# Sliding-window attention and RWKV channel mix on one core: batch 3 joins the batches that are transposed by the DMA crossbar, with a new instruction order

## The chip, the core and the metric

The kernel runs on one core of a Trainium2 chip. The metric is the device time of one execution in microseconds (us), and of several executions their median. One further execution was recorded by the hardware profiler; it has a time of its own and a span, which is the part of it between the first and the last recorded instruction. The engines are named as the profile names them: PE (matrix multiply, with PEld for its weight loads), DVE (vector), ACT (scalar and activation), POOL (GpSimd, here mostly an issuer of software DMAs) and SP (sync, an issuer of hardware DMAs).

## The reference

The input is q, k and v of 8 batches, 8 heads, 576 positions and 64 channels, in float32. The output has the shape (8, 576, 512).

```python
scores = q @ k.T / 8                     # per batch and head, 576 x 576
rel    = i - j
scores = where(0 <= rel < 128, scores - slope[h] * abs(rel), -1e9)
attn   = softmax(scores)
x      = (attn @ v).transpose(0, 2, 1, 3).reshape(8, 576, 512)

x_prev = x shifted by one position (zero at the start of a batch)
xk = mu_k * x + (1 - mu_k) * x_prev
xr = mu_r * x + (1 - mu_r) * x_prev
k  = relu(xk @ w_k) ** 2                 # w_k: 512 x 1024
v  = k @ w_v                             # w_v: 1024 x 512
r  = sigmoid(xr @ w_r)                   # w_r: 512 x 512
out = r * v
```

## The kernel before

**Attention.** A batch is worked on in two halves `c` of four heads, and each half in two groups, so that a batch has four groups `g` of two heads. Matrix operands are bf16. POOL loads q and k with software DMAs as they lie into one of two `raw` buffers (L561, four loads a batch: q and k of each half), and v into one of two `vs` buffers (L540, L545). DVE turns `raw` into `qt` with 32x32 block transposes (L1150, four a batch from batch 1 on). PE makes the scores in 32-row tiles (L1173, function `scores4`), ACT takes the exponential (L1190), DVE multiplies by the mask, which holds window and ALiBi factors (L1200). PE multiplies with v (L796, function `attend`), DVE takes the reciprocal of the sums (L802) and writes the scaled result of a group, positions on the partitions, to one of four `xu` buffers (L807).

**From positions to channels.** The channel mix needs x with its channels on the partitions, in one of two `xt` buffers (one for even batches, one for odd). There are two ways from `xu` to `xt`, and the set `XO` picks the batches of the second. In the first, `out_t`, PE transposes the five 128x128 blocks of a group against an identity matrix into PSUM (L834), and ACT copies the result to `xt` (L710). In the second, `out_flip`, SP issues one DMA that passes through the transposing crossbar, from `xu` to `xt` for all five blocks (L882); the text calls it a flip. In both cases DVE makes the difference of neighbours `dl` (L860) and from it `xk` and `xr` (L867, function `shift`).

**Channel mix.** It works on pairs of batches (0 and 1, 2 and 3, ...), 1152 positions in chunks: 512 when the even batch is there, 384 and 256 when the odd one is; the first pair's 512 are done as 256 and 256. PE multiplies xk by w_k (L949), ACT takes the relu (L956), the square is made on ACT (L920) or DVE (L922), PE multiplies xr by w_r (L967), ACT takes a tanh (L974), from which the sigmoid follows, PE multiplies by w_v (L983), DVE makes the product `ot` (L988), and SP stores rows of 128 positions (L1013); the last 128 columns are stored by ACT (L1007). The number of hardware DMAs, `n_hw`, is rounded up to a multiple of 8 by storing the last rows in two halves each (`n_split` of them).

**The gate.** Ahead of batch b's raw loads, if batch b-2 is in `XO`, POOL copies one element of each group of batch b-2's `xt` to a scratch tile `gap` (L653, function `gate_load`). POOL works in order, so these loads and everything behind them on POOL are held until the flips of batch b-2 have landed.

```python
if GATED and what == "a" and b - 2 in XO:
    gate_load(b)
```

**The order.** All steps are nodes of a list scheduler (class `Plan`) that runs ahead of the launch, in Python. It takes for each engine, whenever that is free by modelled costs, the ready node with the lowest priority value for which buffers are free. Where a node may go to ACT or DVE (the squares, some copies), it goes to the one that the scheduler finds free first. The priority of a node comes from `rank`: its place in the program, moved by tables for each engine (`LEAD` by batch, `SHIFT` by kind of step) and by `NUDGE`, which holds a number for each of some thousand nodes by its running number. `WAIT` puts certain 64-row transposes of PE back, `COST` scales modelled DMA costs, and `FX` is an extra latency that the scheduler adds to the flips of each batch. The engines then carry out exactly the order that the scheduler found, each waiting on semaphores where an operand or a buffer is not there yet. A wrong modelled cost thus shows on the chip as a wait at a fixed place in the order.

Of the kernel before, what the change touches and what calls it, by code (L numbers as in the profile page):

```python
# [182 lines left out]
def kernel(  # L183
# [14 lines left out]
    B, H, S, D = q.shape  # L198
# [16 lines left out]
    XO = range(4,B)  # L215
# [15 lines left out]
    FX = (0, 4, 4, 4, 4, 4, 0, 0)  # L231
# [3 lines left out]
    WAIT = 5.15  # L235
# [90 lines left out]
    def dve_t(n, fast=1):  # L326
# [4 lines left out]
        PE: (379.11, 948.28, 321.48, 777.92, 344.48, 715.92, 627.75, 578.6, 241.8, 354.15),  # L331
        ACT: (700.83, 2.12, 322.35, 108.16, 185.72, -3.46, 340.58, 397.46, 747.05, 580.68),
        DVE: (282.18, -111.4, 162.81, 61.6, 37.49, 18.01, -37.8, -38.84, 70.95, -86.71),
# [3 lines left out]
        PE: {(0, 0): -1189.02, (3, 0): 492.42, (2, 0): 367.63, (1, 0): 298.05, (1, 1): -728.2, (1, 2): 117.95, ('p1', 'fxk'): -1.92, ('rl', 'fp1'): -1166.05, ('frl',): 219.95, ('rs', 'fp1'): 514.38, ('p1', 'fkk'): 4.9, ('fkk',): 426.5, ('ot', 'fp1', 'frs'): 532.6, ('fp1', 'frs'): -626.2},  # L337
        ACT: {(0, 0): -688.81, (3, 0): -610.15, (2, 0): -722.11, (1, 0): 289.16, (1, 1): -432.67, (1, 2): 1038.71, ('p1', 'fxk'): 478.01, ('rl', 'fp1'): 76.23, ('frl',): 491.94, ('rs', 'fp1'): -82.07, ('p1', 'fkk'): -497.1, ('fkk',): 342.85, ('ot', 'fp1', 'frs'): -48.3, ('fp1', 'frs'): 278.04},
        DVE: {(0, 0): -195.31, (3, 0): 34.28, (2, 0): 73.75, (1, 0): 36.73, (1, 1): -73.62, (1, 2): 45.06, ('p1', 'fxk'): 69.74, ('rl', 'fp1'): 265.96, ('frl',): 137.45, ('rs', 'fp1'): -180.96, ('p1', 'fkk'): -389.9, ('fkk',): 250.87, ('ot', 'fp1', 'frs'): -277.33, ('fp1', 'frs'): 509.68},
    }  # L340
    NUDGE = {
# [930 lines left out]
```

## Time and profile before

| | us |
|---|---|
| median of 3 runs | 228.47 |
| lowest, highest | 228.15, 228.95 |
| profiled execution, its time | 227.53 |
| profiled execution, its span | 225.8 |
| PE busy | 217.1 (96%) |
| DVE busy | 196.3 (87%) |
| ACT busy | 166.6 (74%) |
| POOL busy | 59.7 (26%) |

The granted clock of PE was 0.997 of full speed. Busy times of PE count overlapping matmuls up to their modelled ends, so that a stretch in which PE is busy throughout may still have room in it; what an instruction costs PE in a row of others is read from the starts of neighbours in the timeline. In a row of the groups, the columns are the line, engine, operation, operands and count, then the busy time in us and the mean of one in ns, then the idle time ahead of it and what ended that.

### The profile page before, as it was taken

Reading aid. Unit: us, or ns where it says so; the run is one execution under the profiler, and the core shown is the slowest. Engines: PE = TensorE matmul, PEld = TensorE weight load, DVE = VectorE, ACT = ScalarE, POOL = GpSimd, SP = SyncE. Lnnn points to the kernel's source line nnn. Section 1 sums busy time; section 2 is a strip of 40 time slices with the busy share of each in tenths; the row PEclk is TensorE's granted clock in tenths of the full one; section 3 lists DMA queues with packets and bytes.
Section 4 is the critical chain, followed back from the end, with each engine's and each line's share of the span. In section 5 each row is a group of like instructions: output and inputs, shape, how many; then the busy total and the mean of one; then the engine's idle time right before and its main releaser. Section 6 shows DMA issues by size and latency. Waiting matters only on the chain.

```text
span 225.8 us, 5825 instructions
## 1 busy us (share of the span) xinstructions
PE 217.1 (96%) x2339; PEld 128.5 (57%) x2339; DVE 196.3 (87%) x386; ACT 166.6 (74%) x311; POOL 59.7 (26%) x88
## 2 busy tenths in 40 slices
PE   8999978999999999999999999999999999999993
PEld 8576636755756555554774546445674455456542
DVE  7388999999999999999999999999989966983332
ACT  3669999766999789978996796677996684427511
POOL 8776525465100910160007500091000000000000
PEclk9999999999999999999999999999999999999998
DMA  6999999999971997095434995489991315140023
GB/s 157 182 165 195 202 153 207 192 175 233 208 162 49 83 197 179 3 130 88 151 77 58 219 190 108 106 130 188 165 112 29 144 46 121 39 154 37 3 93 139
DMA packets 66298, 29.74 MB, mean 132 GB/s; under 512 B 53976, under 2 KB 58336, under 8 KB 66272
## 3 DMA queue, kind: packets, MB, share of 16 engines
q0 software_dynamic: 46832, 16.26, 66.9%
q1 hardware_dynamic: 17696, 12.53, 20.5%
q10 hardware_dynamic: 1744, 0.59, 1.0%
q8 instruction: 18, 0.29, 0.5%
q14 instruction: 8, 0.07, 0.1%
HBM read 33.56 MB, written 9.44 MB: 190 GB/s over the span
## 4 chain that ended last, share of the span: by engine, by line
PE 80%; DVE 8%; ACT 6%; DMA 3%; issue 1%; SPq 1%; DVEq 0%; ACTq 0%
PE uno L949 25%; PE uno L983 25%; PE uno L967 12%; PE duo L796 7%; PE duo L1173 6%; DMA qx<-in_q_dram 3%; DVE xu L807 2%; DVE qt L1150 2%; ACT at L1190 2%; PE uno L834 2%; PE uno L701 1%; DVE xk L867 1%; ACT mask L1130 1%; ACT at L754 1%; DVE xr L867 1%
## 5 line engine op out<-in xcount | busy, mean ns | idle before, releaser
L949 PE MATMUL uno<-xk,wk_sb 128*128 128x256 bf16 (+2 forms) x416 | 71.3, 314 | 1.7 <-DVE xk L867 1.3
L983 PE MATMUL uno<-wv_sb,kk 128*128 128x512 bf16 (+2 forms) x296 | 68.4, 374 | 0.0
L1190 ACT ACTIVATE at<-duo 128x1024 bf16<-128x1024 f32 x56 | 55.3, 1038 | 12.5 <-PE duo L1173 12.3
L956 ACT ACTIVATE rl<-uno 128x256 bf16<-128x256 f32 (+2 forms) x104 | 47.7, 483 | 14.1 <-PE uno L949 12.8
L949 PEld LDWEIGHTS <-wk_sb 128*128 128x128 bf16 x416 | 38.6, 98 | 24.1 <-issue 3.0
L983 PEld LDWEIGHTS <-kk 128*128 128x128 bf16 x296 | 27.2, 98 | 30.1 <-issue 1.9
L540 POOL DMA_DIRECT2D vs<-in_v_dram x32 | 28.5, 903 | 38.9 <-PE duo L796 29.9
L1200 DVE TENSOR_TENSOR at<-at,mask 128x1024 bf16<-128x1024 bf16 x56 | 37.1, 679 | 1.0 <-ACT at L1190 1.0
L967 PE MATMUL uno<-wr_sb,xr 128*128 128x512 bf16 x144 | 35.9, 379 | 0.0
L974 ACT ACTIVATE rs<-uno 128x512 bf16<-128x512 f32 x36 | 22.0, 618 | 18.5 <-PE uno L967 17.5
L920 ACT ACTIVATE kk<-rl 128x256 bf16<-128x256 bf16 (+2 forms) x67 | 33.7, 530 | 0.8
L1150 DVE STREAM_TRANSPOSE qt<-raw 128x576 f32<-128x576 f32 x28 | 33.7, 1233 | 0.0
L988 DVE SCALAR_TENSOR_TENSOR ot<-rs,uno 128x512 f32<-128x512 bf16 (+2 forms) x37 | 24.0, 663 | 6.7 <-ACT rs L974 4.6
L867 DVE SCALAR_TENSOR_TENSOR xr<-dl,mu_sb,xt 128x576 bf16<-128x576 bf16 (+1 forms) x32 | 24.6, 774 | 0.1
L867 DVE SCALAR_TENSOR_TENSOR xk<-dl,mu_sb,xt 128x576 bf16<-128x576 bf16 (+1 forms) x32 | 24.5, 774 | 0.0
L807 DVE TENSOR_TENSOR xu<-duo,rc 128x640 bf16<-128x640 f32 x28 | 22.8, 818 | 1.5 <-PE uno L834 0.8
L796 PEld LDWEIGHTS <-at 128*128 128x128 bf16 x576 | 21.6, 98 | 4.4 <-issue 0.3
L967 PEld LDWEIGHTS <-xr 128*128 128x128 bf16 x144 | 13.4, 98 | 13.6 <-issue 0.2
L922 DVE TENSOR_TENSOR kk<-rl 128x256 bf16<-128x256 bf16 (+2 forms) x37 | 12.2, 334 | 8.7 <-ACT rl L956 8.0
L796 PE MATMUL duo<-vs,at 128*128 128x65 bf16 x448 | 18.9, 193 | 0.0
L1173 PE MATMUL duo<-qt 32*128 32x256 bf16 (+2 forms) x560 | 18.0, 250 | 0.7 <-ACT at L1190 0.4
L1173 PEld LDWEIGHTS <-qt 32*128 32x128 bf16 x560 | 11.9, 92 | 11.5 <-issue 9.7
(73 smaller groups left out, 160.4 us busy)
## 6 DMA issues: line engine op xcount, KB each, us to landing
out_dram<-ot SPq DMA_DIRECT2D x34, 256.0 KB, 2.8
vs<-in_v_dram POOLq DMA_DIRECT2D x32, 128.0 KB, 10.0
raw<-in_q_dram POOLq DMA_DIRECT2D x14, 288.0 KB, 8.2
raw<-in_k_dram POOLq DMA_DIRECT2D x14, 288.0 KB, 9.3
wk_sb<-in_moe_w_k_dram POOLq DMA_DIRECT2D x2, 512.0 KB, 7.5
wv_sb<-in_moe_w_v_dram POOLq DMA_DIRECT2D x2, 512.0 KB, 11.5
qx<-in_k_dram ACTq DMA_DIRECT2D x4, 128.0 KB, 5.1
qx<-in_q_dram SPq DMA_DIRECT2D x4, 128.0 KB, 4.8
```

The lines of the kernel that those rows point to most:

```text
L540: return dma(POOL, 256, issue_t(1024), lambda e: nc.gpsimd.dma_start(out=vs_buf[h.idx][:, j, :, 0:D], in_=v[b, :, 128 * j:128 * j + 128].r ...
L796: nc.tensor.matmul(a[:, hl, t - t0], lhsT=at[:, lo:lo + 128], rhs=vs[:, u, 2 * g + hl, :] if u < NF else tvb[:, 2 * g + hl], start=(u == u ...
L867: lambda e: nc.vector.scalar_tensor_tensor(out=buf[hk.idx][:, g, e0 + c0:e0 + c1], in0=dls(), scalar=mu[:, g:g + 1], in1=xc(1), op0=ALU.mu ...
L920: nc.scalar.activation(out=out, in_=in_, func=AF.Square)
L949: nc.tensor.matmul(one(hp)[:, 0:n], lhsT=wk_sb[:, po, 128 * fo:128 * fo + 128], rhs=xk_buf[hx.idx][:, po, c0:c1], start=(po == 0), stop=(p ...
L956: a = op(ACT, act_t(n), [s], pr, lambda e, hp=hp, hr=hr: nc.scalar.activation(out=rl_buf[hr.idx][:, 0:n], in_=one(hp)[:, 0:n], func=AF.Rel ...
L967: nc.tensor.matmul(one(hp), lhsT=xr_buf[hx.idx][:, po, 128 * c:128 * c + 128], rhs=wr_sb[:, po], start=(po == 0), stop=(po == NPO - 1))
L983: nc.tensor.matmul(one(hv)[:, a:b], lhsT=kk_buf[hk.idx][:, fo, o:o + 128], rhs=wv_sb[:, fo, a:b], start=(fo == 0), stop=(fo == NFO - 1))
L1150: nc.vector.transpose(out=qt_buf[hq.idx][:, S * i:S * i + S].rearrange("p s t -> p (s t)").bitcast(FP32) .rearrange("p (q t) -> p t q", t=TB),
L1173: nc.tensor.matmul(two(hps[j // 2])[:, j % 2, c0:c0 + n], lhsT=qt[r:r + 32, S + 128 * u:S + 128 * u + 128, t], rhs=qt[r:r + 32, q0:q0 + n, t],
L1190: lambda e, ah=ah, j=j: nc.scalar.activation(out=ah(), in_=two(hps[j]), func=AF.Exp, scale=float(scale)), (), [hps[j]])
L1200: nc.vector.tensor_tensor(out=a, in0=a, in1=m, op=ALU.mult)
```

## The change

Batch 3 joins `XO`: its four groups are transposed by four flips instead of 20 transposes on PE and four copies on ACT. From the rule of the gate it follows that POOL now holds the raw loads of batch 5 until the flips of batch 3 have landed. The scheduler's extra latency `FX` for the flips of batches 1 to 5 becomes 1 us instead of 4, `WAIT` becomes 18.69, and `LEAD`, `SHIFT` and `NUDGE` are replaced as a whole.

```diff
-    XO = range(4,B)
+    XO = range(3,B)
...
-    FX = (0, 4, 4, 4, 4, 4, 0, 0)
+    FX = (0, 1, 1, 1, 1, 1, 0, 0)
     GATED = True
     FWAIT = 6.0
     NO = 6
-    WAIT = 5.15
+    WAIT = 18.69
...
     LEAD = {
-        PE: (379.11, 948.28, 321.48, 777.92, 344.48, 715.92, 627.75, 578.6, 241.8, 354.15),
...
+        PE: (6.12, 274.96, 234.95, 550.78, 273.84, 399.79, 421.2, 620.48, 182.95, 221.81),
...
     NUDGE = {
-        647: 0.01, 648: 0.07, 649: -124.77, 650: 2447.77, 653: -1992.2, 654: 467.14, 656: -664.08, 657: 1548.42, 658: 924.49, 659: 1746.98, 662: 539.28, 663: 1622.07,
...
```

What the emitted instructions are, before and after:

| engine, line | before | after |
|---|---|---|
| PE L834 transposes | 80 | 60 |
| ACT L710 copies to `xt` | 20 | 16 |
| copies to `qk` on ACT, on DVE | 7, 5 | 6, 6 |
| squares on ACT (L920), on DVE (L922) | 67, 37 | 77, 27 |
| SP L882 flips | 16 | 20 |
| POOL L653 gates | 2 | 3 |
| SP L1013 stores | 37 | 41 |

`n_hw` goes from 63 to 67, so that the last five full rows are stored in halves where one was. The orders on PE, DVE and ACT differ almost throughout, from the first batch on.

More of the change, by code (lines that the diff above doesn't have):

```diff
@@ L330 @@
     LEAD = {
-        PE: (379.11, 948.28, 321.48, 777.92, 344.48, 715.92, 627.75, 578.6, 241.8, 354.15),
-        ACT: (700.83, 2.12, 322.35, 108.16, 185.72, -3.46, 340.58, 397.46, 747.05, 580.68),
-        DVE: (282.18, -111.4, 162.81, 61.6, 37.49, 18.01, -37.8, -38.84, 70.95, -86.71),
+        PE: (6.12, 274.96, 234.95, 550.78, 273.84, 399.79, 421.2, 620.48, 182.95, 221.81),
+        ACT: (-210.27, 186.16, 37.99, 143.25, 6.52, 176.03, -94.26, -107.46, -244.5, 375.75),
+        DVE: (-63.33, 29.15, 113.59, 47.57, -49.26, -55.77, -57.59, -42.47, -213.14, 188.34),
     }
@@ L336 @@
     SHIFT = {
-        PE: {(0, 0): -1189.02, (3, 0): 492.42, (2, 0): 367.63, (1, 0): 298.05, (1, 1): -728.2, (1, 2): 117.95, ('p1', 'fxk'): -1.92, ('rl', 'fp1'): -1166.05, ('frl',): 219.95, ('rs', 'fp1'): 514.38, ('p1', 'fkk'): 4.9, ('fkk',): 426.5, ('ot', 'fp1', 'frs'): 532.6, ('fp1', 'frs'): -626.2},
-        ACT: {(0, 0): -688.81, (3, 0): -610.15, (2, 0): -722.11, (1, 0): 289.16, (1, 1): -432.67, (1, 2): 1038.71, ('p1', 'fxk'): 478.01, ('rl', 'fp1'): 76.23, ('frl',): 491.94, ('rs', 'fp1'): -82.07, ('p1', 'fkk'): -497.1, ('fkk',): 342.85, ('ot', 'fp1', 'frs'): -48.3, ('fp1', 'frs'): 278.04},
-        DVE: {(0, 0): -195.31, (3, 0): 34.28, (2, 0): 73.75, (1, 0): 36.73, (1, 1): -73.62, (1, 2): 45.06, ('p1', 'fxk'): 69.74, ('rl', 'fp1'): 265.96, ('frl',): 137.45, ('rs', 'fp1'): -180.96, ('p1', 'fkk'): -389.9, ('fkk',): 250.87, ('ot', 'fp1', 'frs'): -277.33, ('fp1', 'frs'): 509.68},
+        PE: {(0, 0): 297.38, (3, 0): 1113.42, (2, 0): 521.84, (1, 0): -377.65, (1, 1): 856.68, (1, 2): -69.93, ('p1', 'fxk'): 3.79, ('rl', 'fp1'): 1.24, ('frl',): 358.06, ('rs', 'fp1'): -387.28, ('p1', 'fkk'): 9.85, ('fkk',): -922.26, ('ot', 'fp1', 'frs'): 372.44, ('fp1', 'frs'): -394.34},
+        ACT: {(0, 0): -765.86, (3, 0): 144.19, (2, 0): -721.65, (1, 0): 378.01, (1, 1): -765.29, (1, 2): -916.92, ('p1', 'fxk'): -589.65, ('rl', 'fp1'): 285.23, ('frl',): -590.01, ('rs', 'fp1'): 344.07, ('p1', 'fkk'): -377.33, ('fkk',): 236.86, ('ot', 'fp1', 'frs'): -280.47, ('fp1', 'frs'): -1162.35},
+        DVE: {(0, 0): -665.73, (3, 0): -1.5, (2, 0): 10.46, (1, 0): -644.08, (1, 1): -120.65, (1, 2): 8.7, ('p1', 'fxk'): 60.25, ('rl', 'fp1'): 259.93, ('frl',): 405.89, ('rs', 'fp1'): 1355.82, ('p1', 'fkk'): 327.04, ('fkk',): -628.15, ('ot', 'fp1', 'frs'): -478.16, ('fp1', 'frs'): -331.64},
     }
     NUDGE = {
[72 rows of a table removed]
[72 rows of a table added]
     }
```

143 rows, old and new, of the table NUDGE are left out of this document.

## The prediction

> **What bounds the kernel now.** I read the page's busy shares and slices first, then the stages by windows, then the chain that ended last, and then the rows of what the change touches.
>
> ```profile
> span 225.8 us, 5825 instructions
> PE 217.1 (96%) x2339; PEld 128.5 (57%) x2339; DVE 196.3 (87%) x386; ACT 166.6 (74%) x311; POOL 59.7 (26%) x88
> PE   8999978999999999999999999999999999999993
> DVE  7388999999999999999999999999989966983332
> ACT  3669999766999789978996796677996684427511
> ```
>
> PE is at nine tenths or more in nearly every slice, and DVE in most slices too until about 180 us. Which of the two ends the waits is read from the windows (columns: stretch, its length, then PE, PEld, DVE, ACT, POOL) and from the chain (start, length, what).
>
> ```profile
> 50.00:60.00 10.00, 9.46 (x94) 5.84 (x93) 10.00 (x16) 7.78 (x18) 4.67 (x8) 1.00 1.58 222
> 60.00:80.00 20.00, 20.00 (x246) 11.81 (x245) 19.23 (x33) 17.40 (x35) 6.37 (x9) 1.00 0.82 114
> ...
> 51.40 1.47 DVE xk L867 x2
> 54.87 3.47 PE uno L949 x24
> ...
> 218.82 1.51 PE uno L983 x8
> ```
>
> Up to about 53 us the chain runs through loads, DVE and ACT; at 52.9 us PE waits for the last time, 0.47 us, for DVE's fourth `xk` of batch 1 (I call such a point the handover of a batch). From 60 us PE is full in every window and the chain stays on PE until 221 us. So the end is: time of the handover of batch 1, plus PE's work behind it, plus a tail of some 3.5 us. DVE has only 0.4 to 0.9 us idle in each 20 us until 180, so it is next in line.
>
> **The change part by part.** The rows of the operations that are exchanged (by form, and by line for the crossbar transposes; after the bar busy us and mean ns):
>
> ```profile
> L834 PE MATMUL uno<-ident,xu 128*128 128x128 bf16 x80 | 7.3, 220 | 1.2 <-DVE xu L807 1.2
> L710 ACT COPY xt<-uno 128x576 bf16<-128x576 bf16 x12 | 7.8, 661 | 1.5 <-PE uno L834 1.5
> L882 SPq DMA_TRANSPOSE xt<-xu x16: 1200/1210/2662, 110.0 to 195.7; - x16
>   POOL gap L653: 18.8, 1
> DMA to landing us min/median/max: 2.6/2.7/3.4
> 46.16 0.72 PE L834 MATMUL uno<-ident,xu 128*128 128x128 bf16 x10
> 106.62 1.89 DVE L1200 TENSOR_TENSOR at<-at,mask 128x1024 bf16<-128x1024 bf16 x3
> 122.47 0.57 POOL L561 DMA_DIRECT2D raw<-in_k_dram  x1
> ```
>
> *PE.* Matmuls overlap, so 220 ns is a latency. In the timeline ten transposes start at 46.16 and the next matmul at 46.72: 56 ns of PE each. The change removes 20 of them (x80 becomes x60): 20 x 56 ns = 1.1 us, nearly all on the path. I put every PE instruction at its issue step from the timeline (216 ns for 512 columns, 162 for 384, 108 for 256, 30 for the attend matmuls, 0.57 us for a group of scores, 0.1 us for each change to and from its 32-row tiles) and added them in both orders: 203.9 us before, 202.8 after. Behind the handover of batch 1 there are 166.4 us before and 164.8 after: the new order also has 0.4 us more of PE's work ahead of that point. If the handover stays where it is, the end comes 1.6 us earlier.
>
> [...]
>
> *ACT.* Four copies of 661 ns go (2.6 us), ten squares come back from DVE (67 to 77 on ACT, 0.44 to 0.66 us each, some 5 us), one `qk` copy goes to DVE. By step sums ACT grows by 1.5 us, to about 173 us, and has idle time in every window from 60 us on (1.5 to 9 us of 20). I cost this at nothing. If the cover fails, it is in 80 to 120 us, where ACT is at 18 of 20.
>
> *DVE.* Steps from the timeline (three mask products L1200 in 1.89 us, so about 0.61 each; L867 0.73; L1150 1.09; L988 0.60; L807 0.74; L860 0.37; squares 0.21 to 0.34). In sum 194.5 before, 192.5 after: ten squares fewer. But up to the handover of batch 1 it is 46.3 before and 46.7 after: one L1150 more (+1.1) and a `qk` copy (+0.6), against three squares (-0.6) and one L988 fewer (-0.6). Against these +0.4 stands the start, where the copies are dealt out anew; following loads, copies, scores and first exps by hand I get the first attend 0.5 us earlier, give or take 0.5. I take the handover as unmoved, within 0.5 either way.
>
> *Between handovers.* For each handover and mask product I compared DVE's sum up to it with PE's sum up to its first user, counted from the handover of batch 1. Before, DVE keeps at least 0.3 us of room everywhere. After, two points lie below nothing: a mask product of batch 2 (-0.41) and the last `xk` of batch 2 (-0.36), and up to about 110 us there are points with 0.17 to 0.27. DVE also stood idle some 0.7 us for others in that stretch before. So I expect PE to stand for 0.4 at least and 1.1 at most there, and take 0.6. What is late then is PE, on the mask product and on `xk`.
>
> *Flips* (the crossbar transposes, L882). Four more, each 1.2 us of issue on SP (longest 2.66) and 2.7 us to landing (longest 3.4). SP only has stores besides: the stores of pair 0 are all ahead of batch 3's flips, four stores follow. In the new DVE order `dl` of a flipped group stands far enough behind its `xu` for all four (0.5 to 1.6 us of room), and the third `xu` takes the first flip's buffer with 0 to 0.2 us of wait. For batch 4 the fourth `xu` takes the buffer of the first flip back, as only three buffers rotate; I get 0.65 us of DVE wait. The planner's extra latency falls from 4 us to 1, which is less than the 3.9 measured for issue and landing, so such waits are not in its plan. Before, DVE waited 2.4 us for flips in all, and PE for none of it, as it had room of over 3 us at the handovers by then. I charge PE 0.2 us (0 to 0.65).
>
> *The gate.* POOL now holds batch 5's raw loads until batch 3's last flip has landed. Queued behind it on POOL are those four loads and `v` of batch 5; DVE's transposes L1150 of batch 5 wait for them. In before, the gate of batch 6 starts at 119.76 and its last raw load lands 12.2 us later (about 9.5 us from its issue). In after, counting from the end of the last `xu` of batch 3: SP is 0.5 us behind, the gate opens 2.9 later (as for batch 7 before), 12.2 to the last landing: 15.6. DVE needs that load after 4 L860, 8 L867, 8 L1200, 4 L988 and one L1150, 15.6 us by the steps, plus its waits in between. Room 0 to 0.9, as against 1.1 for batch 6 before. I charge nothing, with an open end above (a rival). A gain is excluded: before, these loads went out at 77.4 us, some 20 us ahead of need.
>
> *Stores.* Four more half stores at the end, off the last one; the last squares, L983, L974, L988 and stores stand as before. Nothing.
>
> **Sum.** -1.6 (PE's work) + 0.6 (DVE late up to 110 us) + 0.2 (flips) = -0.8 us. On the profiled execution, 227.53 us (span 225.8), that gives 226.7; it lies 0.9 below the median of 228.47, so by the median 227.7. Terms at their ends: -1.6 - 0.5 + 0.4 = -1.7, and -1.6 + 0.5 + 1.1 + 0.65 = +0.65. About 0.3% (0.69 us) is what a measurement of this kernel can tell from no change.
>
> **Rivals.**
> *The saving comes whole.* PE's removed work and an earlier start both reach the end: -1.6 to -2.1, 226.4 to 226.9. For it: PE is the chain from 53 to 221 us. Against it: the two points below nothing.
> *DVE becomes the bound to 110 us.* If DVE picks up the same 0.7 us idle time that it had before between the handovers of batches 1 and 2, PE stands 0.4 + 0.7 in each of the places without room, and the handover is 0.4 late: -1.6 + 1.1 + 0.4 = -0.1, 228.4. For it: DVE at 10.00 of 10 from 50 to 60 us.
> *Slower: batch 5's loads come late behind the gate.* With the longest landing of a raw load in the trace (11.2 us) in place of 9.5 and no room, DVE stands 1.7 us at L1150 of batch 5, with the 0.65 of batch 4's `xu` behind it; PE's cover there is 0.3 us. -0.8 + 1.7 + 0.65 - 0.3 = +1.3, 229.7; with the longest issue and landing of a flip as well (2.66 and 3.4, together 2.2 more) 231.9. It decides from where the last raw load lands over 16 us after the last `xu` of batch 3. For it: no room in the sum, and software loads that took 4.1 to 11.2 us. Against it: the first and second load of a gated batch land early, and the one that counts was in time for batches 6 and 7.
> [...]
> *The change doesn't do what it says.* Excluded: the new order lists 20 flips, 60 transposes on PE and 3 gates.
>
> **How the numbers follow.** Forecast 0.40; whole saving 0.14; DVE as the bound 0.18; late loads 0.24; something unforeseen in a wholly new order 0.04. Of the forecast's 0.40, 0.28 lies beyond 0.69 us of gain, the rest within. Faster: 0.28 + 0.14 = 0.42. Same: 0.12 + 0.15 = 0.27. Slower: 0.24 + 0.04 + 0.03 of the DVE rival = 0.31. The range goes from 226.5 (most of the whole saving) to 230.2 (late loads a little beyond their first price). The likeliest case by itself: 226.8 to 229.1.
>
> **What would show it.** PE's last wait and its place: if the handover of batch 1 lies near 52.9 us and the later waits for `xk` and masks sum to about 0.6, each step holds. If PE never stands behind 60 us and the end is unmoved, the removed work was misjudged. Waits of POOL's gap for xt<-xu at three places; DVE's L1150 idle <-DMA raw around 100 to 112 us decides the slower rival; DVE's xu idle <-DMA xt<-xu gives the buffer wait. The forecast is wrong if PE stands over 1.5 us behind 60 us, or if the handover moved by over 0.5.

## The result, and the profile after

The changed kernel is slower: 230.12 us in the median of 20 runs against 227.93 us of the kernel before, also 20 runs; the ratio is 1.0088, with a 95% interval of 1.0063 to 1.0113, that is 2.0 us. The ratios here and below leave out executions that took over 1.5% longer than the fastest of their kernel (here one of 231.88 us) and are not worked out from the medians, so the two can differ by some tenths of a microsecond. The profiled execution took 230.18 us, with a span of 228.2 in place of 225.8.

The page of the changed kernel, span, busy times and slices (the last line is the granted clock of PE in tenths):

```profile
span 228.2 us, 5790 instructions
PE 215.5 (94%) x2291; PEld 127.1 (56%) x2319; DVE 195.4 (86%) x377; ACT 167.7 (74%) x316; POOL 61.0 (27%) x89
PE   8898957999999999999998999999999999999994
...
PEclk9999988999999999999999999999999999999998
```

PE has a hole in the sixth slice (28.5 to 34 us), and the clock is lower in that slice and the next; the kernel before had a shallower hole (7 tenths) and the clock at 9 in every slice but the last. The windows, first one of the kernel before, then those of the changed kernel, and the pieces of the chain that are new:

```profile
28.00:32.00 4.00, 2.79 (x48) 1.50 (x40) 4.00 (x8) 3.66 (x7) 1.33 (x3) 1.00 2.55 157
```

```profile
28.00:32.00 4.00, 1.46 (x41) 1.09 (x42) 4.00 (x8) 3.27 (x8) 1.08 (x2) 1.00 2.45 157
32.00:36.00 4.00, 3.95 (x26) 1.49 (x26) 3.69 (x8) 3.12 (x5) 1.74 (x3) 0.57 1.72 178
...
32.40:35.80 3.40, 3.40 (x24) 1.19 (x23) 3.22 (x7) 2.52 (x5) 1.23 (x3) 0.50 1.61 184
...
60.00:80.00 20.00, 19.84 (x214) 11.87 (x214) 19.66 (x32) 19.68 (x40) 5.26 (x7) 1.00 0.80 114
...
120.00:140.00 20.00, 18.88 (x187) 9.59 (x190) 19.57 (x32) 15.49 (x25) 7.34 (x10) 1.00 1.08 150
```

```profile
55.10 3.81 PE uno L949 x24
...
91.32 4.03 DMA xt<-xu
...
114.99 5.34 DMA xt<-xu
```

In each line the figure ahead of the last two is the granted clock: 0.57 from 32 to 36 us, of which 3.4 us at 0.50 (32.4 to 35.8 us), behind four microseconds in which PE was busy for 1.46 (2.79 before). The chain reaches the long L949 of batch 1 at 55 us in place of 53, and where it was PE's alone behind that point, it now goes through two flips. The rows of what the change exchanges:

```profile
L834 PE MATMUL uno<-ident,xu 128*128 128x128 bf16 x60 | 5.9, 222 | 0.0
L710 ACT COPY xt<-uno 128x576 bf16<-128x576 bf16 x8 | 5.1, 643 | 0.1
L882 SPq DMA_TRANSPOSE xt<-xu x20: 1199/1213/2242, 89.9 to 193.9; - x20
  DVE xu L807: 3.2, 2
DMA to landing us min/median/max: 2.6/2.6/5.3
```

The 20 transposes are gone from PE, and DVE now waits 3.2 us, twice, for a flip to give an `xu` buffer back (0.5 us, once, in the kernel before).

Where the time went is read from three points of the timelines: the handover (the first 128x384 group of L949, batch 1; in the new order it follows four matmuls of 256 columns, 0.43 us behind the start of the row at 55.03), the last group of L967, and the end of the span.

| profiled execution | handover | last L967 | between | span |
|---|---|---|---|---|
| before | 52.9 | 220.2 | 167.3 | 225.8 |
| after | 55.5 | 222.8 | 167.3 | 228.2 |
| after, two edits (a_fill_xu4, below) | 54.1 | 219.6 | 165.5 | 224.9 |

The handover is 2.6 us late, and the 1.6 us that PE was to save behind it are spent again, since PE has waits there that it did not have: from 60 to 220 us it is idle for 2.8 us, and for none before. The tail is as before.

### The profile page after: what moved, and what is told of

It reads as the page before. It is cut to its first block, busy times and chain, and to the rows that moved or that the text cites. A ratio compares the mean times of both kernels' runs of the same rounds, so it can differ in the third digit from the quotient of the medians.

```text
span 228.2 us, 5790 instructions
## 1 busy us (share of the span) xinstructions
PE 215.5 (94%) x2291; PEld 127.1 (56%) x2319; DVE 195.4 (86%) x377; ACT 167.7 (74%) x316; POOL 61.0 (27%) x89
## 4 chain that ended last, share of the span: by engine, by line
PE 80%; DMA 7%; DVE 5%; ACT 4%; issue 2%; SPq 1%; DVEq 0%; ACTq 0%
PE uno L949 25%; PE uno L983 25%; PE uno L967 13%; PE duo L1173 6%; PE duo L796 6%; DMA xt<-xu 4%; DMA qx<-in_q_dram 3%; ACT at L1190 2%; PE uno L834 2%; DVE ot L988 1%; PE uno L796 1%; DVE xk L867 1%; PE duo L727 1%; PE uno L701 1%; PE duo L740 1%
## 5 line engine op out<-in xcount | busy, mean ns | idle before, releaser
L949 PE MATMUL uno<-xk,wk_sb 128*128 128x256 bf16 (+2 forms) x411 | 70.5, 313 | 0.6 <-DVE ot L988 0.3
L983 PE MATMUL uno<-wv_sb,kk 128*128 128x512 bf16 (+2 forms) x282 | 67.5, 374 | 1.5 <-DVE kk L922 0.5
L956 ACT ACTIVATE rl<-uno 128x256 bf16<-128x256 f32 (+2 forms) x104 | 47.2, 476 | 14.1 <-PE uno L949 13.2
L949 PEld LDWEIGHTS <-wk_sb 128*128 128x128 bf16 x416 | 38.7, 98 | 23.6 <-issue 1.7
L920 ACT ACTIVATE kk<-rl 128x256 bf16<-128x256 bf16 (+2 forms) x77 | 37.9, 521 | 0.7
L967 PE MATMUL uno<-wr_sb,xr 128*128 128x512 bf16 x135 | 36.2, 390 | 0.5
L974 ACT ACTIVATE rs<-uno 128x512 bf16<-128x512 f32 x36 | 21.5, 605 | 19.8 <-PE uno L967 18.5
L1150 DVE STREAM_TRANSPOSE qt<-raw 128x576 f32<-128x576 f32 x28 | 34.0, 1240 | 0.0
L540 POOL DMA_DIRECT2D vs<-in_v_dram x32 | 28.5, 908 | 20.0 <-PE duo L796 12.4
L867 DVE SCALAR_TENSOR_TENSOR xk<-dl,mu_sb,xt 128x576 bf16<-128x576 bf16 (+1 forms) x32 | 24.5, 772 | 0.1
L867 DVE SCALAR_TENSOR_TENSOR xr<-dl,mu_sb,xt 128x576 bf16<-128x576 bf16 (+1 forms) x32 | 24.5, 772 | 0.1
L796 PEld LDWEIGHTS <-at 128*128 128x128 bf16 x576 | 21.1, 98 | 5.3 <-issue 1.7
L967 PEld LDWEIGHTS <-xr 128*128 128x128 bf16 x144 | 13.5, 99 | 15.0 <-issue 1.3
L796 PE MATMUL duo<-vs,at 128*128 128x65 bf16 x448 | 18.2, 194 | 1.3 <-ACT at L1190 1.3
L922 DVE TENSOR_TENSOR kk<-rl 128x256 bf16<-128x256 bf16 (+2 forms) x27 | 8.8, 330 | 12.0 <-ACT rl L956 11.5
```

Of the source, the lines that this page charges most:

```text
L540: return dma(POOL, 256, issue_t(1024), lambda e: nc.gpsimd.dma_start(out=vs_buf[h.idx][:, j, :, 0:D], in_=v[b, :, 128 * j:128 * j + 128].r ...
L796: nc.tensor.matmul(a[:, hl, t - t0], lhsT=at[:, lo:lo + 128], rhs=vs[:, u, 2 * g + hl, :] if u < NF else tvb[:, 2 * g + hl], start=(u == u ...
L867: lambda e: nc.vector.scalar_tensor_tensor(out=buf[hk.idx][:, g, e0 + c0:e0 + c1], in0=dls(), scalar=mu[:, g:g + 1], in1=xc(1), op0=ALU.mu ...
L920: nc.scalar.activation(out=out, in_=in_, func=AF.Square)
L949: nc.tensor.matmul(one(hp)[:, 0:n], lhsT=wk_sb[:, po, 128 * fo:128 * fo + 128], rhs=xk_buf[hx.idx][:, po, c0:c1], start=(po == 0), stop=(p ...
L956: a = op(ACT, act_t(n), [s], pr, lambda e, hp=hp, hr=hr: nc.scalar.activation(out=rl_buf[hr.idx][:, 0:n], in_=one(hp)[:, 0:n], func=AF.Rel ...
```

## The experiments

All edits of the changed kernel but a_sq, a_pe3 and a_fx4 leave the order of its instructions as it is, and all but a_fx4 act on the finished list of nodes, just before it is emitted.

**Clock and buffers.** Two causes were put apart in one set: the lowered clock at 32 us, and the flips that hold `xu` buffers. `bank` is a free PSUM bank.

```diff
 # a_fill: PE's wait ahead of the second group of scores of batch 1
+for _ in range(8):
+    nc.tensor.matmul(one(bank)[:, 0:512], lhsT=ident, rhs=wk_sb[:, 0, 0:512], start=True, stop=True)
 # a_xu4: xu buffers in turn from batch 3 on, n_xu counts the groups
+h.idx = (n_xu - 16) % NX
 # a_nogate5
+gates[5].emit = None
```

a_fill: 

> The changed kernel with eight idle matmuls (identity by w_k, 512 columns, into a free PSUM bank, result not used) put into the 2.3 us in which PE waits ahead of the second group of scores of batch 1. Nothing else is moved. Theory 1 (the clock): PE's idle stretch of 28.9 to 31.2 us makes the granted clock fall to 0.55 to 0.60 in 32 to 36 us; with the stretch filled the clock stays at 1.00, the matmuls L967 of 31.75 take 1.9 us in place of 3.0, and the time falls by 1.3 to 1.6 us, to 1.002 to 1.003 of the kernel before. Theory 2 (ACT sets the start): the slow matmuls lie beside exps that are awaited anyway; the time falls by less than 0.5 us. In either the wait for the exp itself stays.

a_xu4: 

> The changed kernel, order untouched, with the four xu buffers taken in turn from batch 3 on, in place of the lowest free one by the plan. Theory 1 (buffers): the 3.2 us in which DVE waits for xu <- DMA xt<-xu go to under 0.5, and as DVE has no room left up to 130 us the time falls by 1.2 to 1.8 us. Theory 2 (cover): PE has room of 3 us and more against DVE by the handovers of batches 3 and 4, so the waits are hidden, and the time changes by less than 0.4 us.

a_fill_xu4: 

> Both edits. If the clock and the buffers are the two causes, they add: 2.5 to 3.3 us less than the changed kernel, 226.9 to 227.6 where the kernel before is 227.9, that is 0.995 to 0.999 of it. If both were hidden: no change from the changed kernel, 1.009.

a_nogate5: 

> The changed kernel, order untouched, without the gate ahead of batch 5's raw loads, which then go out at about 78 us as in the kernel before. Theory 1 (collision): the first flip of batch 4, 5.3 us to landing at 115 us, shares the DMA engines with batch 5's q, k and v, which the gate moved to 100 to 115 us; without the gate it lands in about 3 us, DVE's second wait for an xu buffer shrinks from 1.7 to 0.5 or less, and the time falls by 0.3 to 1.0 us. Theory 2 (late loads, the slower rival of the prediction): DVE's transposes L1150 wait for these loads; as the profile of the changed kernel shows no idle time ahead of L1150, this gives nothing. Theory 3: the flips are slow because of each other, and landing stays at 4 to 5 us; time within 0.3 us.

| run | median us (runs) | ratio to before, interval |
|---|---|---|
| a_fill | 230.92 (6) | 1.0129, 1.0089 to 1.0169 |
| a_xu4 | 228.30 (12) | 1.0015, 0.9994 to 1.0036 |
| a_fill_xu4 | 228.59 (12) | 1.0020, 0.9996 to 1.0044 |
| a_nogate5 | 229.59 (6) | 1.0083, 1.0050 to 1.0116 |

The buffers count for what the first theory said: from 1.0088 to 1.0015, 1.7 us. Its row of `xu` has lost the wait for flips, though the second flip of batch 3 still takes 4.0 us to land, as in the changed kernel; it is slow, but no `xu` waits for it.

```profile
L807 DVE TENSOR_TENSOR xu<-duo,rc 128x640 bf16<-128x640 f32 x28 | 22.3, 813 | 0.4 <-PE uno L834 0.2
```

a_fill missed: its time did not fall. In its profile the mechanism is there. First the timeline of PE in the changed kernel, then in a_fill:

```profile
31.18 0.64 PE L1173 MATMUL duo<-qt 32*128 32x256 bf16 x24 [2.34 <-ACT at L1190]
31.75 3.00 PE L967 MATMUL uno<-wr_sb,xr 128*128 128x512 bf16 x7
```

```profile
31.44 0.64 PE L1173 MATMUL duo<-qt 32*128 32x256 bf16 x24 [0.65 <-ACT at L1190]
32.02 1.90 PE L967 MATMUL uno<-wr_sb,xr 128*128 128x512 bf16 x8
```

L967 runs at full clock again: the granted clock is 1.00 from 32 to 36 us, 0.57 in the changed kernel. The handover comes 43.5 us behind the first attend in place of 44.6, so the fill is worth 1.1 us there; by the clock time it is 0.8 us earlier, as this execution started 0.3 us later. But DVE then waited 5.3 us for `xu` buffers in four places, against 3.2 in two: an earlier PE arrives earlier at buffers that are not free. With the buffers in turn as well (a_fill_xu4), these waits are gone. And one filled wait does not settle the clock. Every run so far has a mean granted clock, and they fall in two groups, 0.983 to 0.993 and 0.997 to 1.000. Of the runs of the new order with no wait filled (changed kernel, a_xu4, a_nogate5), 32 of 38 are in the lower group; with one filled, 10 of 18. In a_xu4 the lower group has a median of 228.4 us and the two others 227.1 and 227.4, so it costs about 1.1 us; in the changed kernel 1.8 (230.25 against 228.47, the one of 231.88 left out).

a_fill_xu4 missed what was expected of it: its median is no lower than that of a_xu4. Its runs are split by the clock, seven at 228.70 us and five at 227.25 in the median; the five are where the expectation had put all of them.

a_nogate5 left the first wait for a buffer (1.7 us, 1.5 in the changed kernel) and took the second: the first flip of batch 4, issued at 115.5 us, has landed when DVE starts the fourth `xu` at 119.1 without a wait, so within 3.6 us in place of 5.3, as the theory of a collision had it. But the flips of batch 3 now take 2.9 to 5.6 us (2.6 to 4.0 before the edit), and the ratio went down by 0.0005 only, within the intervals. On the time the run is inconclusive, and the question was put again below.

**Three waits filled, the price of a transpose, and the flips by themselves.**

```diff
 # a_fill3_xu4 (with a_xu4): scores group 2, attend groups 1 and 2 of batch 1
+fill(scores[1], 11); fill(attend[0], 4); fill(attend[1], 2)
 # a_fill3_xu4_t40: ahead of eight groups of L949 from 100 us on
+for i in range(5):
+    nc.tensor.transpose(one(h).bitcast(BF16)[:, 128 * i:128 * i + 128], wk_sb[:, 0, 128 * i:128 * i + 128], ident)
 # b_flip3: kernel before, batch 3, in the place of PE's transposes
+nc.sync.dma_start_transpose(out=xt..., in_=xu...)
 # b_fill: kernel before, waits of PE at 28 to 35 us
+fill(out_t, 5); fill(mix[0], 1); fill(mix[1], 1)
```

a_fill3_xu4: 

> The changed kernel with the xu buffers in turn and idle matmuls in three waits of PE: 11 ahead of the second group of scores of batch 1 (28 to 31 us), 4 and 2 ahead of the first two attend groups of batch 1 (34.4 to 36.7 us). So far the runs with a mean clock of 0.992 take 1.1 to 1.4 us longer than those with 0.998 to 1.000, and with the first wait alone filled 10 of 18 still had it (32 of 38 unfilled). Theory 1 (idle PE in 28 to 37 us lowers the clock): nearly all runs have 0.998 or more, median 226.9 to 227.3, 0.996 to 0.999 of the kernel before. Theory 2 (the clock falls for another reason or at another place): share and median as with one wait filled, 228.6.

a_fill3_xu4_t40: 

> The same with 40 idle transposes of 128x128 on PE added in the stretch from 100 us on, five ahead of each of eight groups of L949, into the bank that the group overwrites; results not used. [...]

b_flip3: 

> The kernel before, its order on PE, ACT, DVE and POOL untouched, but the four groups of batch 3 flipped on SP in the place where PE's transposes stood (and the four copies of ACT gone), xu buffers in turn from batch 3 on, stores split as in the changed kernel, no gate for batch 5. In the kernel before, dl of batch 3 stands 3.0 to 3.5 us behind the end of its xu, and a flip takes 3.9 us. Theory 1 (the flips as such pay): DVE waits some 1 to 2 us in all at dl, which its room against PE by then covers, PE is 1.1 us shorter: 0.5 to 1.1 us faster than before, 0.995 to 0.998. Theory 2 (the flips as such cost): the waits reach PE, 0 to 1 us slower than before.

b_fill: 

> The kernel before with idle matmuls in PE's waits between 28 and 35 us (5, 1 and 1). 7 of 23 runs of the kernel before had a mean clock of 0.992 or less and took 228.3 in the median against 227.4. Theory 1 (idle PE lowers the clock): fewer than 1 in 10 has it, and the median falls by 0.1 to 0.3 us. Theory 2 (another place or reason): share and median stay.

| run | median us (runs) | ratio to before, interval | clock 0.995 or less |
|---|---|---|---|
| a_fill3_xu4 | 227.66 (12) | 0.9996, 0.9972 to 1.0020 | 0 of 12 |
| a_fill3_xu4_t40 | 229.14 (12) | 1.0060, 1.0037 to 1.0082 | 0 of 12 |
| b_flip3 | 237.33 (7) | 1.0386, 1.0341 to 1.0430 | 7 of 7 |
| b_fill | 227.60 (12) | 0.9988, 0.9964 to 1.0011 | 0 of 12 |
| before, beside these | 227.67 (29) | 1 | 7 of 29 |

On the clock the first theory holds in both orders: none of these 36 runs with filled waits has the low clock. (b_flip3 loses it elsewhere: its profile has 1.00 from 28 to 36 us, but 0.91 from 80 to 100 and 0.83 from 100 to 120 us, the stretches in which the chain goes through the late flips of batch 3.) What a run without them gets is a matter of chance, 32 of 38 in the new order and, over the first two sets, 14 of 52 in the old. The median of b_fill fell by only 0.07 us, which can't be told from nothing. The median of a_fill3_xu4 is what b_fill and the kernel before have, 0.4 us above the range expected of it: filled waits and free buffers bring the change back to the kernel before and no further.

The 40 idle transposes (their results are not used) cost 1.5 us (229.14 against 227.66), not the 2.2 that 40 steps of 56 ns would make. In the timeline each five take 0.28 us, 56 ns each, as the prediction had it:

```profile
102.98 0.44 PE L1283 MATMUL uno<-ident,wk_sb 128*128 128x128 bf16 x5
103.26 0.60 PE L949 MATMUL uno<-xk,wk_sb 128*128 128x256 bf16 x4
```

So 37 ns of 56 reach the end, or 0.75 us for 20. Part of the rest may be seen in the profiles: PE's two later waits in a_fill3_xu4, 0.4 and 0.2 us, are gone in the other.

b_flip3 was expected to gain a little, and lost about 9 us (8.8 by the ratio; 9.3 by the medians without its two longest runs). The flips of batch 3 landed late, and DVE stands at `dl` for each of them (the edit shifts the lines by 7: L867 is the L860 of the other kernels):

```profile
L867 DVE TENSOR_TENSOR dl<-xt 128x576 bf16<-128x576 bf16 x28 | 12.3, 446 | 10.7 <-DMA xt<-xu 10.7
```

```profile
DMA to landing us min/median/max: 4.7/6.2/8.9
```

The expectation had reckoned with 3.9 us. The profiled execution is one of the two longest, 239.75 us, so the sizes of its waits are on the high side. Here the raw loads of batch 5 go out at 77.5 us and its v at 99.5, ahead of the flips and between them, and no gate holds anything. What the flips would cost in this order with a gate was not run.

**The gate, the flips in the new order, and the start.** All three have the buffers in turn and the three waits filled.

```diff
 # a_sq: three squares L920 ahead of batch 1's first exp go behind its second
+order[i_:i_] = early
 # a_pe3: batch 3, three PE steps behind the place of the flip; gate of batch 5 out
+for t in range(NJ): nc.tensor.transpose(tp_[:, 128 * t:128 * t + 128], xu..., ident)
+copy_any(ACT, xt..., tp_[:, 0:S])
 # a_nogate5_xu4
+gates[5].emit = None
```

a_sq: 

> The kernel with xu in turn and three waits filled, and on ACT three squares L920 that stand ahead of the first two exps of batch 1 moved behind them. ACT of the changed kernel makes 6 squares before 29 us where the kernel before makes 4, and its first exp L1190 starts at 29.1 in place of 28.4 us. Theory 1 (ACT's squares hold up the start): the exps start about 0.5 us earlier and PE's first 128x384 group of batch 1 too; 0.3 to 0.7 us less than without the move (227.66), 0.996 to 0.999 of the kernel before. Theory 2 (the new order has 0.4 us more PE work ahead of that point and waits elsewhere): less than 0.2 us.

a_pe3: 

> The kernel with xu in turn and three waits filled, but batch 3 back on PE and ACT: five transposes a group and a copy of 128x576, put three PE steps behind where the flip was issued; no gate for batch 5, all else in the new order. Theory 1 (the flips of batch 3 pay in the new order): 0.7 us (37 ns each, as the 40 idle ones cost) to 1.1 us (56 ns) more than with the flips. Theory 2 (they pay nothing, as DVE or ACT sets the pace there): within 0.3 us. Theory 3 (the flips cost, by DVE's waits for them and by the collision with loads): faster without them by 0.3 us or more.

a_nogate5_xu4: 

> The kernel with xu in turn and three waits filled, without the gate of batch 5. If the gate acts only through the buffers that late flips keep, it is worth nothing once the buffers are taken in turn: within 0.3 us. If early loads slow the flips of batch 3 so that dl waits for them (4.7 us to landing in the run without the gate), it is 0.3 to 1 us slower.

| run | median us (runs) | ratio to before, interval |
|---|---|---|
| a_sq | 227.97 (12) | 0.9989, 0.9966 to 1.0013 |
| a_pe3 | 228.70 (12) | 1.0011, 0.9986 to 1.0036 |
| a_nogate5_xu4 | 229.67 (9) | 1.0076, 1.0045 to 1.0107 |
| before, beside these | 228.43 (25) | 1 |

In this set 15 of the 25 runs of the kernel before had the low clock, so its median is higher; its runs with the full clock have 227.6 us (227.3 in the set ahead). Against those, a_fill3_xu4 stands at +0.35 us and a_pe3 at +1.1: taking the flips of batch 3 away, and their gate with them, costs 0.7 us, or 1.0 by the plain medians. Theory 1: the flips pay, and about as much as the idle transposes say. That it is the transposes alone is not shown: the four copies are back on ACT too, and in the profile DVE waits 2.7 us for exps, 0.5 in a_fill3_xu4.

The gate is worth 2 us (229.67 against 227.66; 1.7 when each is held against the runs at full clock in its own set), well over the 0.3 to 1 expected. Without it DVE waits for `dl`, and the flips of batch 3 are slow, with loads beside them: in a_nogate5 four loads of v go out from 93 to 96 us, between flips issued from 89.8 to 96.4. First the wait (of the whole execution) and the landing of the flips from 85 to 105 us in a_nogate5_xu4, then the landing with the gate, in a_fill3_xu4:

```profile
DVE dl L860 <- DMA xt<-xu: 4.2, 3, 1.9
...
DMA to landing us min/median/max: 4.2/6.1/7.7
```

```profile
DMA to landing us min/median/max: 2.6/3.2/4.3
```

a_sq took 227.97 us, no less than the 227.66 without the move, but it doesn't acquit ACT's squares. The exps do start earlier, 0.7 us behind the first scores in place of 1.1. The eleven idle matmuls that fill PE's wait, though, run as long as before, and the second scores come right behind them:

```profile
28.64 2.55 PE L1262 MATMUL uno<-wk_sb,ident 128*128 128x512 bf16 x11
31.12 0.64 PE L1173 MATMUL duo<-qt 32*128 32x256 bf16 x24
```

So the fill takes the place of the wait that the move was to shorten, and a gain of up to 0.4 us could not show. In a_sq one square reads the relu of another block, as a relu is written ahead of it, so its output is not right; the instructions and their sizes are the same, and the time is read for that alone.

**The scheduler's latency.**

```diff
-    FX = (0, 1, 1, 1, 1, 1, 0, 0)
+    FX = (0, 4, 4, 4, 4, 4, 0, 0)
```

a_fx4: 

> The changed kernel with the scheduler's extra latency FX for flips back at 4 us, WAIT, LEAD, SHIFT and NUDGE as in the change; the scheduler then finds another order from batch 3 on. Theory 1 (FX stands for the truth, and 1 us was the mistake that keeps buffers too short): DVE's waits for flips shrink and the time falls by 1 to 2 us against the changed kernel. Theory 2 (the buffer waits come from the modelled length of the transfer, which FX does not enter, and the tables fit one order only): no fewer waits for xu buffers, and a new order that nothing was fitted to, 2 to 6 us slower than the changed kernel.

It took 234.53 us in 4 runs, 1.0294 (1.0243 to 1.0345) of the kernel before, that is 4.4 us above the changed kernel: in time, theory 2. DVE waits less for `xu` buffers, 1.9 us for 3.2, where that theory had no fewer waits, but not less for flips in all, and it and PE wait for other things instead:

```profile
DVE dl L860 <- DMA xt<-xu: 2.0, 2, 1.1
DVE xu L807 <- DMA xt<-xu: 1.9, 1, 1.9
```

## Why the prediction was wrong, step by step

The forecast was -0.8 us, and the kernel is 2.0 us slower.

**PE's work behind the handover, -1.6.** Near enough. With free buffers the stretch takes 165.5 us in a_fill_xu4, 165.6 in a_xu4 and 166.2 in a_fill3_xu4, in place of 167.3. Of this the swap of transposes and copies for flips is 0.7 to 1.0 us by a_pe3, less than the 1.1 that the sum put nearly all on the path for the 20 transposes.

**Handover unmoved, within 0.5.** This failed, by 2.6 us in the profile. The table's step from 55.5 to 54.1 us, when the first wait is filled, is 1.4 us, but 0.3 of that is an earlier start of that execution: from the first attend to the handover it is 44.6 us in the changed kernel and 43.5 in a_fill, a_fill_xu4 and a_fill3_xu4. So 1.1 us are the clock: PE stood 2.34 us for an exp, in a stretch with little else to do, and the clock was granted at 0.50 for 3.4 us behind. The prediction read the clock at 1.00 in the windows that it showed of the kernel before and left it out. The other 1.5 us are the order itself. The sums gave 0.4 more for each of DVE and PE, and set against DVE's a start that would be 0.5 us earlier; the first attend came 0.14 us earlier (10.87 for 11.01), less than executions of the new order differ among themselves (10.27 to 11.13), but the first group of L949 at 19.4 in place of 16.6, and the first scores of batch 1 0.5 us later. The rest arises behind these scores, where PE waits for exps; first the kernel before, then the changed one, up to 56 us:

```profile
PE duo L1173 <- ACT at L1190: 0.4, 2, 0.2
```

```profile
PE duo L1173 <- ACT at L1190: 2.3, 1, 2.3
PE duo L796 <- ACT at L1190: 1.3, 2, 0.8
```

A sum of steps up to a point says nothing of the waits in the chain from exp to scores to exp, and there they decided. Which of the moved steps makes these 1.5 us stays open. By how much earlier the exps start in a_sq, its three squares could be 0.4 of them, and that is not shown.

**DVE late on masks and `xk` up to 110 us, +0.6.** Not seen: PE's waits in the changed kernel name no mask product and no `xk`. Of PE's 2.8 us of idle time behind 60 us, 1.6 are left in a_xu4, and the stretch is 1.7 us shorter there: most of what PE lost came from flips that kept buffers.

**Flips, +0.2 (0 to 0.65).** The term that was sized worst: 3.2 us of DVE's waits, 1.7 us at the end. The prediction named the mechanism for batch 4 (the fourth `xu` takes the first flip's buffer, 0.65) and priced it with a landing of 2.7 us. That row came from the flips of the kernel before, whose longest took 3.4. In the new order two `xu` of batch 3 end 0.7 us apart, and the second of the pair took 4.0 us; batch 4's first flip, beside the loads that the gate had moved to 100 to 115 us, took 5.3, and 3.6 at most without those loads (a_nogate5). For batch 3 the sum looked at the third `xu`, and it was the fourth that waited. The cover that was named, 3 us of room at the handovers, is not there for scores that wait on DVE within a batch.

**The gate, nothing.** The loads came in time: L1150 has no idle time ahead of it, and the rival of late loads didn't happen. That rival had the sign and nearly the size of the result, by another way: the gated loads do harm by slowing a flip of batch 4, 5.3 us with them and 3.6 at most without. On the whole, a_nogate5_xu4 says, the gate does more good than harm once the buffers are free.

**ACT, stores.** For ACT the prediction looked for cover from 60 us on and found it; the waits for exps that cost time lie ahead of that, before the handover, where it looked at DVE and PE alone. The stores cost nothing, as said: the tail from the last L967 to the end of the span is 5.6 us before and 5.4 after.

**What would show it.** "Over 1.5 us behind 60 us, or the handover moved by over 0.5" was the mark of a wrong forecast; both came true, with 2.8 and 2.6 us. The landing of a flip was not one number: 2.6 to 2.7 us for those of batch 4 in the kernel before, with a DMA share of 0.40 from 110 to 118 us, and beside loads 4.2 to 7.7 us in a_nogate5_xu4 and 4.7 to 8.9 in b_flip3.

Account of the profiled execution, from the table above: handover +1.1 (clock) and +1.5 (order), PE's work -1.8, waits for flips +1.8: +2.6 at the last L967, of which 2.4 are left in the span. It compares one execution of the changed kernel at the low clock with one of the kernel before at the full clock; in the medians the clock is mixed on both sides.

## What to carry to other kernels

The landing of a DMA holds for the company in which it was measured (2.6 us for a flip in a quiet stretch here, 4.2 to 8.9 beside loads): before a transfer is put in the place of an engine's work, look up what else is in flight where it will go, and for how long its source buffer is kept. An order that a search has found is part of the kernel: flips dropped into the old one, without a gate, cost about 9 us and a changed latency 4.4, so an operation is priced by taking it out of the order that was made for it. And where PE is the bound, look at the granted clock run by run ahead of comparing medians: the runs at the low clock took 1.1 us longer in a_xu4 and 1.8 in the changed kernel.

## What the runs showed of the hardware

In the changed kernel PE waited for 2.3 us among light work (busy for 1.46 of the 4 us from 28 us on), and then 3.4 us went by at a granted clock of 0.50, from 32.4 us on. In a_xu4 the windows from 28 to 32 and from 32 to 36 us have 0.93 and 0.64, in a_fx4 1.00 and 0.57; reckoned at 0.50, that is an estimated 3.4 us in each, from 31.4 us on in a_xu4 and from 32 us or a little later in a_fx4. One such stretch takes some 0.0075 off the mean clock of a span of 228 us, which is what the runs at 0.992 and 0.993 lack. Whether it happens differs from run to run of the same kernel (16 of 20 runs of the changed kernel; 30 of 84 of the kernel before over four sets, from 1 of 7 to 15 of 25). What decides between them was not shown. Seventeen idle matmuls in the waits removed it all but once: 1 of 57 runs of the new order with three waits filled had the low clock (0.991, in a_nogate5_xu4).
